# Transposes of two units in product banks, an earlier k, h blocks around the last attn x v, and new scheduler clocks, in a fused attention and MLP kernel

## The chip, the cores and the metric

The kernel runs on one core of one Trainium2 chip. The metric is the device time of one execution in microseconds (us). Each comparison runs the kernel before and the changed one in turns on the same chip.

The engines have the names of the profile: PE does the matmuls (x3600 on the page of the kernel before), ACT is the scalar engine (x373), DVE the vector engine (x515). The program gives PE's results tiles in PSUM; a "bank" here is such a tile of 2048 bytes a partition, as in `mm_tile` (512 fp32 columns).

## The reference, cut to what matters

```python
scores = q @ k.transpose(0, 1, 3, 2) / sqrt(64)        # 8 batches, 12 heads, 448 x 64
attn   = maximum(scores, 0) ** 2 / 448
x      = (attn @ v) as [3584, 768]
h      = x @ w_in                                      # 768 x 2048
out    = (maximum(h, 0) ** 2) @ w_out                  # 2048 x 768
```

## The kernel before

Work comes in units: four heads of one batch, three units per batch, 24 in all. A unit has seven score tiles of 128 x 896. PE makes scores into a "slot", which is two PSUM banks. ACT turns a slot into an `at` tile (relu, fp16), DVE squares `at`, and PE multiplies it by v. The output, xt, feeds the "h blocks": six matmuls into one product bank (`mm`). ACT or DVE copies that bank to g, and DVE squares g. The later stages use sums of weights and activations (`s`, `ws`, `x`) so as to need fewer matmuls; DVE makes these sums.

The scores need q^T and k^T. From unit 6 on a transposing DMA makes them; for units 0 to 5 PE does, with an identity matmul:

```python
def slot(dtype):                       # two slots of two banks, a third one in the first 27 us only
    ...
def pe_transpose(n):
    srcs = q16s.pop(n); ts = new_qkt(); ps = slot(FP16)
    def copy(i, eng):                  # eng 0: ACT, else DVE
        ...
    # 14 transposes of q, 14 of k, into the two banks of one slot
    ...
    if n == 3: return lambda: (copy(0, 0), copy(1, 0))
    if n > 0:  copy(0, n < 3); copy(1, n < 3)          # units 4, 5: both on ACT
```

The program for all engines is written out once, in order, by a small scheduler. It keeps two clocks: `at_pe` is its guess of how far PE is, `at_ve` the same for DVE. From these it decides where in DVE's order a square goes:

```python
def put(d):
    ready, cost, fn, _ = d.popleft()
    at_ve[0] = max(at_ve[0], at_pe[0], ready) + cost
    fn()
def fill(until):
    for d in (due, due_g):             # due: squares of at; due_g: relu and square of g
        while d and max(at_ve[0], at_pe[0], d[0][0]) + d[0][1] <= until:
            put(d)
def av_unit():                         # attn x v of a whole unit
    ...
    flush(rest=False)
    at_pe[0] += 2.65
def visit(tiles, ...):                 # scores of one or two tiles
    ...
    at_pe[0] += 0.19 + 0.38 * len(tiles)
```

Of the kernel before, what the change touches and what calls it, by code (L numbers as in the profile page):

```python
# [10 lines left out]
FP16 = mybir.dt.float16  # L11
FP32 = mybir.dt.float32
AF = mybir.ActivationFunctionType
# [4 lines left out]
def kernel(  # L18
# [9 lines left out]
    nc = tc.nc  # L28
# [13 lines left out]
    P = 128  # L42
    J = 7
# [4 lines left out]
    NF = FF // P  # L48
# [21 lines left out]
    PSUM = bass.MemoryType.PSUM  # L70
# [19 lines left out]
    def load16(n):  # L90
        tq = q16_p.tile([P, 2, J * D], FP16, name="q16", tag="q16")
        tk = q16_p.tile([P, 2, J * D], FP16, name="k16", tag="k16")
        nc.gpsimd.dma_start(out=tq, in_=heads(q, n))
        nc.gpsimd.dma_start(out=tk, in_=heads(k, n))
        q16s[n] = (tq, tk)

    def load_v(n):
        t = v_p.tile([P, 2, J * D], FP16, name="vt", tag="vt")
        nc.gpsimd.dma_start(out=t, in_=heads(v, n))
        vts[n] = t  # L100
# [56 lines left out]
    nc.vector.memset(zeros, 0.0)  # L157
    junk = const_p.tile([P, 1], FP16, name="junk", tag="junk")
    nc.scalar.activation(out=junk, in_=zeros[:, 0:1], func=AF.Relu)
    load_v(0)  # L160
    load16(1)
    load_v(1)
    load16(2)
    load_v(2)

    def sums_w1(i):
# [27 lines left out]
    def slot(dtype):  # L194
        slot_no[0] += 1
        third = not big and slot_no[0] % 3 == 2 and slot_no[0] < 29
        return (third_p if third else s_p).tile(
            [P, 2, 2048 // mybir.dt.size(dtype)], dtype, name="slot", tag="slot")
# [7 lines left out]
    def pe_transpose(n):  # L206
        srcs = q16s.pop(n)
        ts = new_qkt()
        ps = slot(FP16)

        def copy(i, eng):
            dst = ts[i].rearrange("p j c -> p (j c)")
            if eng == 0:
                nc.scalar.activation(out=dst, in_=pss[i][:, i, 0:J * P], func=AF.Copy)  # L214
            else:
                nc.vector.tensor_copy(dst, pss[i][:, i, 0:J * P])

        pss = [ps, slot(FP16) if n == 0 else ps]
        for i, src in enumerate(srcs):
            for j in range(J):  # L220
                for hh in range(2):
                    nc.tensor.transpose(  # L222
                        pss[i][64 * hh:64 * hh + 64, i, j * P:(j + 1) * P],
                        src[:, hh, j * D:(j + 1) * D], ident)
            if n == 0:
                copy(i, 1)
                warm(1)
        qkt[n] = ts
        if n == 3:
            return lambda: (copy(0, 0), copy(1, 0))  # L230
        if n > 0:
            copy(0, n < 3)
            copy(1, n < 3)
        return None


    xts: dict = {}
# [49 lines left out]
    def av_some(lag=2, most=3):  # L287
        done = 0
        while av_order and done < most:
            t = av_order[0]  # L290
            if t not in seen or seen[t] > now[0] - lag:
                break
            av_order.popleft()
            av_round(t)
            done += 1
            if t % J == J - 1:
                break
# [3 lines left out]
    def av_unit():  # L301

        n = unit[0]
        if n == NUN or seen.get(n * J + J - 1, 10 ** 6) >= now[0]:
            return
        unit[0] += 1
        flush(rest=False)
        at_pe[0] += 2.65
        b, u = divmod(n, NU)
        vt = vts[n]  # L310
        ps = slot(FP32)
        for j in range(J):
            at = ats.pop(n * J + j)
            for hp in range(2):
                r = slice(64 * hp, 64 * hp + 64)
                for hh in range(2):
                    nc.tensor.matmul(  # L317
                        ps[64 * hh:64 * hh + 64, hp, 0:S],
                        lhsT=vt[r, hh, j * D:(j + 1) * D], rhs=at[r, hh, :],
                        start=(j == 0), stop=(j == J - 1))  # L320
        if u == 0:
            xts[b] = x_p.tile([P, NM, S], FP16, name="xt", tag="xt")
        nc.scalar.activation(
            out=xts[b][:, 2 * u:2 * u + 2, :], in_=ps[:, :, 0:S],
            func=AF.Copy, scale=CX)
# [16 lines left out]
    at_pe = [0.0]  # L342
    at_ve = [0.0]
# [6 lines left out]
# [4 lines that stand above are left out]
# [6 lines left out]
    def now_ve(cost, lag=0.25):  # L360
        at_ve[0] = max(at_ve[0], at_pe[0] + lag) + cost
# [9 lines left out]
    def visit(tiles, turn=None, lag=2, most=3):  # L371
        now[0] += 1
        for t in tiles:
            if t % J == 0 and t >= NPE * J:
                prefetch(t // J + 2)
        if big:
            for t in tiles[:1]:
                score(t)
            av_unit()
            for t in tiles[1:]:  # L380
                score(t)
            at_pe[0] += 0.19 + 0.38 * len(tiles)
            for i, t in enumerate(tiles):
                square(ats[t], 0.6 + 0.85 * i)
            return
        for t in tiles:
            score(t, 2)
        later = pe_transpose(turn) if turn is not None else None
        flush()
        av_some(lag, most)  # L390
        if later:
            later()
        for t in tiles:
            square(ats[t])
        flush()
# [2 lines left out]
    gts: dict = {}  # L398
    mm_no = [0]

    def mm_tile(i=None):
        if i is None:
            mm_no[0] += 1
            i = mm_no[0] % len(big)
        return big[i].tile([P, 512], FP32, name="mm", tag="mm")

    def g_of(b):
        if b // 2 not in gts:
# [3 lines left out]
    def h_group(b, f):  # L412
        z = (b % 2) * S
        cell = [None]

        def step(m):
            def run():
                if m == 0:
                    cell[0] = mm_tile()
                nc.tensor.matmul(  # L420
                    cell[0][:, 0:S],
                    lhsT=w1[f // 4][:, m, (f % 4) * P:(f % 4 + 1) * P],
                    rhs=xts[b][:, m, :], start=(m == 0), stop=(m == NM - 1))
                if m < NM - 1:
                    return
                f0 = f - f % 2
                g = g_of(b)[:, f0:f0 + 2, z:z + S]
                if b == 0 and (f % 2 == 1 or f == 0) and f < 14:
                    nc.vector.tensor_scalar(
                        out=g[:, f % 2], in0=cell[0][:, 0:S],  # L430
                        scalar1=0.0, scalar2=None, op0=ALU.max)
                else:
                    nc.scalar.activation(
                        out=g[:, f % 2], in_=cell[0][:, 0:S], func=AF.Relu)
                flush()
                if b == 0 and f == NF - 1:
                    square(g)
                elif f % 2 == 1:
                    nc.vector.tensor_mul(g, g, g)
            return run  # L440

        return [(0.1892, step(m), m == 0) for m in range(NM)]
# [151 lines left out]
    def sums(i, rows, to):  # L594

        a1, a2 = tile_of(rows[0]), tile_of(rows[1])
        x, y = ((a2[:, LO], a2[:, HI]), (to.get(1), a1[:, LO]),
                (a1[:, LO], a2[:, LO]), (a1[:, HI], to.get(2)))[i - 1]
        to[i] = late["s"].tile([P, KH, P], FP16, name=f"s{i}", tag=f"s{i}")
        op = nc.vector.tensor_add if i == 1 else nc.vector.tensor_sub  # L600
        now_ve(0.6)
        op(to[i], x, y)  # L602

# [169 lines left out]
    NB0 = NU * J  # L773
    warm(10)
    pe_transpose(0)
    for i in range(11):
        visit([t for t in (2 * i, 2 * i + 1) if t < NB0],
              turn={1: 1, 4: 2, 10: 3}.get(i))
        if i == 0:
            load16(3)  # L780
            load_w1(0)
            load_w1(1)
            load_v(3)
        if i == 2:
            load16(4)
            load_w1(2)
            load_v(4)
        if i == 5:
            load16(5)
            load_w1(3)  # L790
            load_v(5)
    load_v(6)
    load_w2(b11, 0, 0)
    load_w2(b12, 0, 1)
# [2 lines left out]
    load_qk(6)  # L797
    load_qk(7)
    first.close()
    big.append(ctx.enter_context(tc.tile_pool(name="mma", bufs=2, space=PSUM)))  # L800


    f0 = h_group(0, 0)
    for _, fn, _ in f0[0:4]:
        fn()
    av_some(0, 9)
    rounds.close()
    big.append(ctx.enter_context(tc.tile_pool(
        name="mmb", bufs=2, space=PSUM, side="right", reuse_waits="tile")))
    visit([NB0, NB0 + 1])  # L810

    T_G = NM * 0.1892
# [31 lines left out]
    for pr in range(1, B // 2):  # L844
# [3 lines left out]
        for i in range(21):  # L848
            ts = [t0 + 2 * i, t0 + 2 * i + 1]
# [25 lines left out]
    for i in (1, 2):  # L875
        events.append((2 * T_H - (3 - i) * T_G, lambda i=i: outs[0][1](i)))

    steps = [(0.1892, None, False)] * 4 + f0[4:]
    for f in range(1, NF):
        steps += h_group(0, f)  # L880
    for f in range(NF):
        steps += h_group(1, f)
# [49 lines left out]
```

## Time and profile before

| | kernel before |
|---|---|
| median of the first three runs | 378.81 us |
| range of these | 378.57 to 378.95 us |
| span of the profiled execution | 377.6 us (its device time was 379.35 us) |
| busy: PE, DVE, ACT | 96%, 74%, 66% |

The device time is some 1.8 us more than the span (379.35 against 377.6 here). A timeline line gives the start, the duration, the engine, the source line, the operation and how many instructions were merged; the bracket gives idle time of the engine before it and what ended it. For PE the duration is modelled (the score pair of the changed kernel at 35.57 us is given 0.57 us, and the next group starts after 0.50), so the text measures from the start of one group to the start of the next. L258 is line 258 of the kernel that was profiled, so the same instruction has another line number in another kernel.

### The profile page before, as it was taken

The numbers are of one execution on the slowest core, as the hardware profiler recorded it, in microseconds if no ns is written. First come the engines' busy times: TensorE is split into PE (matmuls) and PEld (weight loads), VectorE is DVE, ScalarE is ACT, GpSimd is POOL, SyncE is SP. The second block draws the span as 40 slices with busy tenths as digits, with TensorE's granted clock in tenths as the row PEclk, the third lists the DMA queues.
The fourth block names the chain that finished last, engine by engine and source line by source line (L and its number), as shares of the span: only waits on it lengthen the run. The fifth ranks groups of instructions, "written<-read, shape, count | busy, mean of one in ns | idle before, by whom it ended". The sixth has DMA issues, their size and how long they took to land.

```text
span 377.6 us, 8806 instructions
## 1 busy us (share of the span) xinstructions
PE 363.5 (96%) x3600; PEld 231.3 (61%) x3600; DVE 278.6 (74%) x515; ACT 249.8 (66%) x373; POOL 107.1 (28%) x128
## 2 busy tenths in 40 slices
PE   7889999999999999999999999999999999999994
PEld 3544444444455678785555577877555588985663
DVE  1796567997767689897965758989956688995542
ACT  2897996686677798775566578877766785532220
POOL 8545431944440444404042243150000000000001
PEclk9999999999999999999999999999999999999998
DMA  8999999999999999789498997893132200002333
GB/s 120 197 204 205 205 203 177 124 171 134 121 139 187 134 114 139 90 95 82 96 112 134 184 178 68 83 110 63 38 97 69 76 26 2 2 0 65 94 96 84
DMA packets 121160, 42.65 MB, mean 113 GB/s; under 512 B 100832, under 2 KB 117760, under 8 KB 121120
## 3 DMA queue, kind: packets, MB, share of 16 engines
q0 software_dynamic: 82912, 23.01, 59.9%
q1 hardware_dynamic: 38048, 18.98, 26.2%
q8 instruction: 28, 0.46, 0.5%
q10 hardware_dynamic: 160, 0.10, 0.1%
q14 instruction: 12, 0.10, 0.1%
HBM read 45.61 MB, written 11.01 MB: 150 GB/s over the span
## 4 chain that ended last, share of the span: by engine, by line
PE 81%; ACT 6%; DVE 6%; issue 2%; DMA 2%; POOL 1%; POOLq 0%; ACTq 0%; DVEq 0%
PE mm L729 33%; PE mm L550 23%; PE slot L252 9%; PE mm L420 9%; PE slot L317 7%; ACT at L256 4%; DVE at L369 2%; DMA k<-in_k_dram 2%; PE slot L222 1%; DVE g L491 1%; ACT m L486 1%; DVE xt L283 1%; DVE s L602 1%; DVE g L498 0%; ACT qT L214 0%
## 5 line engine op out<-in xcount | busy, mean ns | idle before, releaser
L256 ACT ACTIVATE at<-slot 128x896 f16<-128x896 f32 x168 | 146.2, 920 | 33.0 <-PE slot L252 33.0
L369 DVE TENSOR_TENSOR at<-at 128x896 f16<-128x896 f16 x168 | 99.7, 618 | 15.7 <-ACT at L256 14.5
L108 POOL DMA_DIRECT2D qs<-in_q_dram x36 | 35.4, 984 | 121.3 <-DMA qT<-qs 113.6
L729 PEld LDWEIGHTS <-s 128*128 128x128 f16 x440 | 41.7, 98 | 32.0 <-issue 4.3
L252 PE MATMUL slot<-qT,kT 64*64 64x448 f16 x756 | 58.1, 360 | 2.6 <-ACT at L256 1.2
L550 PEld LDWEIGHTS <-w 128*128 128x128 f16 x576 | 54.4, 98 | 5.9 <-issue 5.4
L550 PE MATMUL mm<-xt,w 128*128 128x224 f16 x432 | 48.6, 259 | 0.0
L729 PEld LDWEIGHTS <-g 128*128 128x128 f16 x336 | 31.5, 98 | 24.0 <-issue 5.0
L550 PEld LDWEIGHTS <-ws 128*128 128x128 f16 x432 | 40.2, 98 | 6.7 <-issue 6.7
L729 PE MATMUL mm<-b,g 128*128 128x384 f16 x224 | 40.7, 326 | 0.0
L420 PE MATMUL mm<-xt,w 128*128 128x448 f16 x192 | 39.6, 353 | 0.3 <-ACT xt L280 0.3
L729 PE MATMUL mm<-b,s 128*128 128x384 f16 x216 | 39.6, 326 | 0.1
L729 PE MATMUL mm<-t,s 128*128 128x384 f16 x224 | 39.5, 326 | 0.0
L636 DVE SCALAR_TENSOR_TENSOR osb<-mm,u 128x384 f32<-128x384 f32 (+1 forms) x30 | 16.2, 541 | 31.2 <-ACT u L631 23.0
L252 PEld LDWEIGHTS <-kT 64*64 64x64 f16 x756 | 19.9, 104 | 31.1 <-issue 25.7
L108 POOL DMA_DIRECT2D ks<-in_k_dram x36 | 35.0, 975 | 9.9 <-DMA b<-in_moe_w_out_dram 5.8
L631 ACT ACTIVATE u<-mm 128x384 f32<-128x384 f32 x28 | 13.7, 491 | 32.6 <-PE mm L729 31.4
L571 POOL DMA_DIRECT2D out_dram<-osb x2 | 1.1, 563 | 120.5 <-DVE osb L636 120.5
L550 PE MATMUL mm<-x,ws 128*128 128x224 f16 x288 | 34.4, 259 | 0.9 <-ACT m L486 0.9
L317 PE MATMUL slot<-at,vt 64*64 64x448 f16 x588 | 32.2, 350 | 0.6 <-DVE at L369 0.5
L498 DVE TENSOR_TENSOR g<-g 128x896 f16<-128x896 f16 x48 | 29.7, 619 | 1.1 <-ACT g L501 0.2
L420 PEld LDWEIGHTS <-w 128*128 128x128 f16 x192 | 17.3, 98 | 19.1 <-issue 4.8
(66 smaller groups left out, 400.2 us busy)
## 6 DMA issues: line engine op xcount, KB each, us to landing
out_dram<-osb SPq DMA_DIRECT2D x52, 192.0 KB, 3.3
vt<-in_v_dram POOLq DMA_DIRECT2D x24, 224.0 KB, 6.6
qs<-in_q_dram POOLq DMA_DIRECT2D x36, 112.0 KB, 4.4
ks<-in_k_dram POOLq DMA_DIRECT2D x36, 112.0 KB, 5.3
w<-in_moe_w_in_dram POOLq DMA_DIRECT2D x8, 384.0 KB, 11.5
b<-in_moe_w_out_dram POOLq DMA_DIRECT2D x4, 768.0 KB, 17.1
q<-in_q_dram POOLq DMA_DIRECT2D x6, 224.0 KB, 8.3
k<-in_k_dram POOLq DMA_DIRECT2D x6, 224.0 KB, 8.6
```

What stands on the lines that cost most here:

```text
L108: nc.gpsimd.dma_start(out=t[:, :, hh, :], in_=heads(src, n)[:, hh].rearrange("p (j d) -> p j d", d=D))
L222: nc.tensor.transpose(pss[i][64 * hh:64 * hh + 64, i, j * P:(j + 1) * P], src[:, hh, j * D:(j + 1) * D], ident)
L252: nc.tensor.matmul(ps[c, hh, 0:S], lhsT=kT[r, j, c], rhs=qT[r, :, c], start=True, stop=True)
L256: nc.scalar.activation(out=at, in_=ps[:, :, 0:S], func=AF.Relu, scale=SK)
L317: nc.tensor.matmul(ps[64 * hh:64 * hh + 64, hp, 0:S], lhsT=vt[r, hh, j * D:(j + 1) * D], rhs=at[r, hh, :], start=(j == 0), stop=(j == J - 1))
L369: lambda: nc.vector.tensor_mul(at, at, at), 0))
L420: nc.tensor.matmul(cell[0][:, 0:S], lhsT=w1[f // 4][:, m, (f % 4) * P:(f % 4 + 1) * P], rhs=xts[b][:, m, :], start=(m == 0), stop=(m == NM ...
L498: due_g.append((t, 0.54, lambda: nc.vector.tensor_mul(g, g, g), b))
L550: nc.tensor.matmul(XY[s][y][:, r * Q:(r + 1) * Q], lhsT=left(k, i0 + 2 * s + r, m), rhs=right(k, m), start=(fresh and r == 0 and m == 0), ...
L631: nc.scalar.activation(out=t, in_=X[0][:, 0:HALF], func=AF.Copy, scale=CO)
L636: nc.vector.scalar_tensor_tensor(out=osb[row][:, c], in0=acc[0][:, 0:cc.stop - cc.start], scalar=CO, in1=keep[nm][:, cc], op0=ALU.mult, op ...
L729: nc.tensor.matmul(acc[0][:, 0:HALF], lhsT=left()[:, f], rhs=right[:, f], start=(fresh and f == 0), stop=(f == KH - 1), skip_group_check=n ...
```

## The change

It has three parts by intent, and a fourth that touches the scheduler's clocks. (1) q and k of unit 1 are loaded ahead of v of unit 0, so that the first transposes don't wait for k. (2) Unit 3 is transposed behind more attn x v work, and the first h blocks stand around the last attn x v, where PE waited for copies. (3) Units 4 and 5 are transposed into two product banks, so that the score slots stay free, and k^T is copied by DVE beside ACT's q^T. (4) The clocks get PE's real times, and squares that are due go ahead of the `s` sums.

```diff
+    load16(1)
     load_v(0)
-    load16(1)
+    load16(2)
     load_v(1)
-    load16(2)
     load_v(2)
 ... pe_transpose
+        if n > 3:
+            pss = [mm_tile(None, FP16).rearrange("p (i c) -> p i c", i=1) for _ in range(2)]
+        else:
+            pss = [ps, slot(FP16) if n == 0 else ps]
 ...
         if n == 3:
-            return lambda: (copy(0, 0), copy(1, 0))
+            return lambda: (copy(0, True), copy(1))
         if n > 0:
-            copy(0, n < 3)
-            copy(1, n < 3)
+            copy(0, n > 3)
+            copy(1)
 ... av_unit, visit, sums
-        at_pe[0] += 2.65
+        at_pe[0] += 1.33
-            at_pe[0] += 0.19 + 0.38 * len(tiles)
+            at_pe[0] += 0.19 + 0.19 * len(tiles)
+        while due and due[0][0] <= max(at_ve[0], at_pe[0]) + 0.3:
+            put(due)
         now_ve(0.6)
 ... main part; turn 3 goes from the last visit to behind the loop
+    later = pe_transpose(3)
 ...
-    for _, fn, _ in f0[0:4]:
-        fn()
+    av_some(1, 9)
+    some(f0[0:2])
+    later()
     av_some(0, 9)
 ...
+    some(f0[2:4])
+    some(f1[0:2])
     visit([NB0, NB0 + 1])
```

More of the change, by code (lines that the diff above doesn't have):

```diff
@@ L208, in pe_transpose, with copy @@
         ts = new_qkt()
-        ps = slot(FP16)
-        def copy(i, eng):
-            dst = ts[i].rearrange("p j c -> p (j c)")
-            if eng == 0:
-                nc.scalar.activation(out=dst, in_=pss[i][:, i, 0:J * P], func=AF.Copy)
-            else:
-                nc.vector.tensor_copy(dst, pss[i][:, i, 0:J * P])
-        pss = [ps, slot(FP16) if n == 0 else ps]
+        ps = None if n > 3 else slot(FP16)
+        def copy(i, act=False):
+            dst, ps = ts[i].rearrange("p j c -> p (j c)"), pss[i][:, i if n < 4 else 0, 0:J * P]
+            if act:
+                nc.scalar.activation(out=dst, in_=ps, func=AF.Copy)
+            else:
+                nc.vector.tensor_copy(dst, ps)
+        if n > 3:
+            pss = [mm_tile(None, FP16).rearrange("p (i c) -> p i c", i=1) for _ in range(2)]
+        else:
+            pss = [ps, slot(FP16) if n == 0 else ps]
         for i, src in enumerate(srcs):
@@ L222, in pe_transpose @@
                     nc.tensor.transpose(
-                        pss[i][64 * hh:64 * hh + 64, i, j * P:(j + 1) * P],
+                        pss[i][64 * hh:64 * hh + 64, i if n < 4 else 0, j * P:(j + 1) * P],
                         src[:, hh, j * D:(j + 1) * D], ident)
             if n == 0:
-                copy(i, 1)
+                copy(i)
                 warm(1)
@@ L229, in pe_transpose @@
         if n == 3:
-            return lambda: (copy(0, 0), copy(1, 0))
+            return lambda: (copy(0, True), copy(1))
         if n > 0:
-            copy(0, n < 3)
-            copy(1, n < 3)
-        return None
+            copy(0, n > 3)
+            copy(1)
     xts: dict = {}
@@ L387, in visit @@
             score(t, 2)
-        later = pe_transpose(turn) if turn is not None else None
+        if turn is not None:
+            pe_transpose(turn)
         flush()
         av_some(lag, most)
-        if later:
-            later()
         for t in tiles:
@@ L399, with mm_tile @@
     mm_no = [0]
-    def mm_tile(i=None):
+    def mm_tile(i=None, dtype=FP32):
         if i is None:
@@ L404, in mm_tile @@
             i = mm_no[0] % len(big)
-        return big[i].tile([P, 512], FP32, name="mm", tag="mm")
+        return big[i].tile(
+            [P, 2048 // mybir.dt.size(dtype)], dtype, name="mm", tag="mm")
     def g_of(b):
@@ L776 @@
     for i in range(11):
-        visit([t for t in (2 * i, 2 * i + 1) if t < NB0],
-              turn={1: 1, 4: 2, 10: 3}.get(i))
+        visit([t for t in (2 * i, 2 * i + 1) if t < NB0], turn={1: 1, 4: 2}.get(i))
         if i == 0:
@@ L799, with some @@
     first.close()
-    big.append(ctx.enter_context(tc.tile_pool(name="mma", bufs=2, space=PSUM)))
-    f0 = h_group(0, 0)
-    for _, fn, _ in f0[0:4]:
-        fn()
+    big.append(ctx.enter_context(tc.tile_pool(
+        name="mma", bufs=2, space=PSUM, reuse_waits="tile")))
+    f0, f1 = h_group(0, 0), h_group(0, 1)
+    def some(part):
+        for _, fn, _ in part:
+            fn()
+    av_some(1, 9)
+    some(f0[0:2])
+    later()
     av_some(0, 9)
@@ L876 @@
         events.append((2 * T_H - (3 - i) * T_G, lambda i=i: outs[0][1](i)))
-    steps = [(0.1892, None, False)] * 4 + f0[4:]
-    for f in range(1, NF):
+    steps = [(0.1892, None, False)] * 6 + f1[2:4] + f0[4:6] + f1[4:6]
+    for f in range(2, NF):
         steps += h_group(0, f)
```

## The prediction

> **What bounds the kernel now.** I read the page first: busy times, then the chain that ended last.
>
> ```profile
> PE 363.5 (96%) x3600; PEld 231.3 (61%) x3600; DVE 278.6 (74%) x515; ACT 249.8 (66%) x373; POOL 107.1 (28%) x128
> PE 81%; ACT 6%; DVE 6%; issue 2%; DMA 2%; POOL 1%; POOLq 0%; ACTq 0%; DVEq 0%
> ```
>
> PE is the bound, with 81% of the chain. The change touches about the first 60 us, so I ask for PE's busy time by stretch (columns: stretch, its length, then busy time and count per engine: PE, PEld, DVE, ACT, POOL; clock, DMA share, GB/s).
>
> ```profile
> 0.00:27.40 27.40, 22.65 (x356) 12.49 (x356) 17.16 (x32) 18.92 (x23) 16.93 (x30) 1.00 1.10 173
> 45.00:60.00 15.00, 14.54 (x140) 6.34 (x138) 10.50 (x20) 13.80 (x18) 3.87 (x4) 1.00 1.55 193
> 60.00:84.00 24.00, 23.96 (x178) 11.29 (x171) 21.65 (x32) 16.98 (x27) 13.37 (x15) 1.00 1.75 155
> ```
>
> Up to 27.4 us PE is not full: there ACT is the bound, turning 21 score tiles into `at`. From 45 to 60 us ACT is nearly as full as PE (13.80 of 15). From 60 to 84 PE is full without a gap, so time won before 60 us moves everything behind it forward. The view of who waits for whom names what the change is aimed at (us in total, times, longest):
>
> ```profile
> PE slot L222 <- ACT at L256: 1.0, 3, 0.6
> PE slot L222 <- DMA k<-in_k_dram: 0.7, 1, 0.7
> PE slot L252 <- ACT kT L214: 0.5, 2, 0.3
> PE mm L420 <- ACT xt L280: 0.3, 1, 0.3
> ```
>
> Busy time alone hides part of the loss, because matmul ends are modelled. So I work from starts in the timeline: a group's real time is the next PE group's start minus its own.
>
> [...] Seven 128-column fp16 transposes are 896 columns, 1792 bytes, so q^T fits one product bank and k^T another; before, both lie in one two-bank score slot, and there are only two such slots after the first 27 us. [...] 0.62 us on DVE, 0.92 on ACT. [...] So the place of a copy in its engine's order matters; the trace shows ACT rows in program order throughout.
>
> **The change part by part.**
>
> (1) *k of unit 1 ahead of v of unit 0.* The first loads form one stream in issue order; the landings in the trace are q0 5.12, k0 6.20, v0 7.40, q1 8.72, k1 11.45, v1 12.63 us, about 1.2 us each with one 2.7 us step at k1. What k1's lateness costs, in the timeline:
>
> ```profile
> 8.42 3.35 ACT L256 ACTIVATE at<-slot 128x896 f16<-128x896 f32 x4 [6.18 <-PE slot L252]
> 10.20 0.58 PE L222 MATMUL slot<-ident,q 128*64 128x128 f16 x14 [0.24 <-ACT at L256]
> 11.49 0.58 PE L222 MATMUL slot<-ident,k 128*64 128x128 f16 x14 [0.72 <-DMA k<-in_k_dram]
> 12.01 0.95 PE L252 MATMUL slot<-qT,kT 64*64 64x448 f16 x16
> 12.63 4.96 ACT L256 ACTIVATE at<-slot 128x896 f16<-128x896 f32 x6 [0.87 <-PE slot L252]
> ```
>
> k1 becomes the fourth load and lands at about 8.7 us (10.3 if the long step stays in that place), both before 10.78, when PE has done the q transposes. Then the k transposes start at 10.78 instead of 11.49, the scores at 11.30 instead of 12.01, and ACT's next tile at 11.92 instead of 12.63; ACT is busy to 11.77, so its gap falls from 0.87 to 0.15. Gain 0.71. ACT bounds this stage to 27.3, and its other gaps (0.34 and 0.27) come from PE waiting for ACT's slots, so they move along: the 0.71 arrives at 27.3. v0 lands at about 11.45, its first use is near 12.1, so it should not take over as a wait, with 0.6 us to spare.
>
> (2) *First h blocks around the last attn x v; q^T, k^T of unit 3 on two engines.* Before:
>
> ```profile
> 26.57 0.58 PE L222 MATMUL slot<-ident,q 128*64 128x128 f16 x14 [0.57 <-ACT at L256]
> 28.83 0.76 PE L270 MATMUL avt<-at,vt 64*64 64x448 f16 x12
> 29.42 0.55 PE L252 MATMUL slot<-qT,kT 64*64 64x448 f16 x8
> 30.22 2.81 PE L420 MATMUL mm<-xt,w 128*128 128x448 f16 x14 [0.25 <-ACT xt L280]
> ```
>
> The score group of 8 before the transposes begins at 25.27 and takes 1.30 us to the next start; undisturbed such a group takes 0.51. The group at 29.42 takes 0.80 (it ends in the wait for xt on ACT, behind both copies). With the small gaps at changes of tile form PE loses 1.67 us between 25.27 and the end of the third h block at 32.96 (7.69 us elapsed, 6.02 of work at 0.047 us per 64x64 matmul of 448, 0.189 per h matmul, 0.033 per transpose). After, 8 attn x v matmuls stand ahead of the transposes and fill 0.4 of the slot wait, and eight h matmuls stand behind the last attn x v while xt is copied, so that wait vanishes. What stays is 0.3 at the slot and some 0.65 of changes of form. Gain about 0.7.
>
> (3) *Units 4 and 5 through product banks.* Before, unit 4:
>
> ```profile
> 35.72 0.92 ACT L214 ACTIVATE qT<-slot 128x896 f16<-128x896 f16 x1 [0.49 <-PE slot L222]
> 36.53 0.91 ACT L214 ACTIVATE kT<-slot 128x896 f16<-128x896 f16 x1
> 37.50 0.38 PE L252 MATMUL slot<-qT,kT 64*64 64x448 f16 x4 [0.26 <-ACT kT L214]
> 37.81 0.87 PEld L420 LDWEIGHTS <-w 128*128 128x128 f16 x6 [0.20 <-issue]
> 39.05 0.88 PE L252 MATMUL slot<-qT,kT 64*64 64x448 f16 x8
> 39.87 0.87 PEld L420 LDWEIGHTS <-w 128*128 128x128 f16 x6 [0.20 <-issue]
> ```
>
> The first score pair behind the transposes starts at 36.85 and takes 0.96 until 37.81: its second tile belongs to unit 3 and does not need k^T, it waits for the slot that the copies still read. The next takes 0.82 (39.05 to 39.87), because ACT is late by the k^T copy. Undisturbed is 0.51, so the loss is 0.45 + 0.31 = 0.76. After, the slot is free and the first term goes. The second stays mostly: ACT must still do the g copy, then two tiles of 0.86 each, while PE reaches the second tile of the next pair 1.4 us or so after the g copy; I leave 0.2 of the 0.31. k^T on DVE stands behind two squares and a g square there, which puts its end some 2 us behind the transposes, about 1 us before the first scores of unit 4. Unit 5 (46.32 to 47.28, 48.52 to 49.34) has the same figures. Gain 2 x 0.55 = 1.1.
>
> (4) *The scheduler's clock* (1.33 and 0.19 for 2.65 and 0.38, and squares put ahead of the `s` sums). The compiled order shows PE unchanged behind 50 us; DVE only swaps neighbours: pairs of squares (1.1 us) move ahead of an `s` sum at some ten places, a few relu and square steps change places. In the trace the sums end 0.6 to 5.8 us before their products. At the tightest place (0.11 us, at 338) the order is unchanged; at the next (0.64, at 265) the sum moves forward. The remaining waits of PE behind 90 us hang on ACT copies, whose order does not change. I count 0, give or take 0.6.
>
> Sum: 0.71 + 0.7 + 1.1 = 2.5 us, 378.8 - 2.5 = 376.3 us.
>
> **The rivals.** *A: the loads take it back.* If the transfers set the pace, an earlier PE only waits. Against: k^T of unit 6, the first one made by a transposing DMA, lands at 65.91 and its first scores start at 71.05, and no later unit has less than 5 us; the last w1 part lands at 40.4 and is used near 54. If v0 landed after 12.1 it would cost part (1) up to 0.7: 377.0. *B: the copy on DVE is late*, behind two squares, and the scores of unit 4 wait for k^T instead of for the slot. For: [...] its slice from 34.8 to 37.0 is solid. Against: the 1 us worked out above. It would cost up to 1.1: 377.4. *C: DVE's new order starves something behind 84 us*, where it is 74% to 90% busy: a few waits of 0.3 to 0.6 more, 377 to 378; or fewer, 375.3. *D: the waits removed were shadows of ACT's load*, which stays nearly full from 45 to 60 us: then part (3) gives just the 0.45 twice, or less, and the total is 376.6 to 377.
>
> **Range and chances.** A 2% step is 7.6 us, three times the whole sum; all PE waits of the first 60 us together would not reach it, and no part adds work to PE. Range 375.2 to 377.6: the low end has 0.5 more from ACT's relief and 0.6 from part (4), the high end loses one whole part. Faster by 2%: 0.01; within: 0.98; slower: 0.01.
>
> **What would show each step right or wrong.** (1) No wait on k in PE's waits, ACT's gap before its fifth tile near 0.15. (2) The wait for xt on ACT gone, the third h block done near 31.5. (3) The wait for ACT kT gone, the pair behind the transposes at 0.51, the next pair near 0.7. At 62 us the same h matmul 2.5 us earlier, and the distance kept to the end. (4) is wrong if that lead grows or shrinks by over 0.6 behind 84 us. A wait on v0, on kT from DVE or on a product bank would make the prediction wrong.

The traces show:

- The changed kernel copies q^T and k^T of unit 4, 128 x 896 in fp16 (1792 bytes), each out of one product bank (`qT<-mm` at 34.05 us, `kT<-mm` at 35.68); the program gives that tile 2048 bytes.
- The figures 0.62 and 0.92 us in the prediction are copies of 896 columns out of a slot in the trace of before: its six on DVE (L216) took 0.61 to 0.63 us, its six on ACT (L214) 0.91 to 0.92.
- All 373 instructions of ACT and 515 of DVE in the trace of before, and 370 and 518 in that of the changed kernel, stand in the order of the compiled program (compared by their source lines). That is what the argument on places in an engine's order rests on.
- For the "changes of form": an h block of six between groups of another tile form takes 1.24 us (33.47 to 34.71 in the trace of before), where six times 0.189 is 1.13; 14 h matmuls in a row take 2.74 (30.22 to 32.96), where the work is 2.65. So it is some 0.1 us for a group, of six or of 14. A score pair takes 0.51 (32.96 to 33.47), where its work is 0.38.
- By the view of stretches DVE is busy 72% to 86% from 84 to 341 us in the trace of before; the 74% to 90% of rival C is a little high.

## The result, and the profile after

The changed kernel took 377.69 us (median of six, 377.66 to 378.12), the kernel before 378.69 us on the same chip (378.51 to 379.09). The ratio is 0.9975, with a 95% interval of 0.9962 to 0.9988. A ratio here is the mean time of one kernel's fast runs over that of the other's in the same rounds, so it is not quite the ratio of the medians. The change gains 1.0 us; the prediction said 2.5, with a range that ended at 377.6.

The page of the changed kernel, the lines of busy time and of the chain that ended last:

```profile
PE 363.3 (97%) x3600; PEld 231.1 (61%) x3600; DVE 280.4 (75%) x518; ACT 247.6 (66%) x370; POOL 107.2 (29%) x128
PE 80%; DVE 9%; ACT 6%; issue 2%; DMA 1%; POOLq 0%; POOL 0%; ACTq 0%; DVEq 0%
```

DVE's share of the chain has grown from 6% to 9%. Its busy time has grown by only 1.8 us, which is its three new copies of k^T (some 0.6 us each). A view by stretch shows that early on ACT has been relieved and PE is fuller (from 45 to 60 us ACT 12.83 us after 13.80 before, PE 14.69 after 14.54):

```profile
45.00:60.00 15.00, 14.69 (x144) 6.59 (x137) 9.74 (x18) 12.83 (x18) 3.87 (x4) 1.00 1.53 194
60.00:84.00 24.00, 24.00 (x175) 11.54 (x174) 23.13 (x35) 17.84 (x29) 11.17 (x12) 1.00 1.68 139
```

Part (1) in the timeline. The wait of 0.72 us before the k transposes is gone, they follow q's at once, and ACT runs from its first tile without a gap (seven tiles in one line):

```profile
8.50 5.84 ACT L258 ACTIVATE at<-slot 128x896 f16<-128x896 f32 x7 [6.26 <-PE slot L254]
10.28 0.58 PE L225 MATMUL slot<-ident,q 128*64 128x128 f16 x14 [0.24 <-ACT at L258]
10.66 0.58 PE L225 MATMUL slot<-ident,k 128*64 128x128 f16 x14
```

Part (2). The scores of unit 3 now take 0.51 us (28.80 to 29.31), since nothing waits for xt any more. The third h block ends at 31.68, so the stretch that took 7.69 us before takes 7.24 (24.44 to 31.68):

```profile
24.44 0.72 PE L254 MATMUL slot<-qT,kT 64*64 64x448 f16 x8
25.73 0.58 PE L225 MATMUL slot<-ident,q 128*64 128x128 f16 x14
28.80 0.57 PE L254 MATMUL slot<-qT,kT 64*64 64x448 f16 x8
29.31 2.44 PE L422 MATMUL mm<-xt,w 128*128 128x448 f16 x12
31.68 0.57 PE L254 MATMUL slot<-qT,kT 64*64 64x448 f16 x8
```

Part (3), unit 4. The pair of score tiles behind the transposes takes 0.50 us (35.57 to 36.07) in place of 0.96. The next pair takes 0.89 (37.31 to 38.20), not less than the 0.82 of before but more:

```profile
35.57 0.57 PE L254 MATMUL slot<-qT,kT 64*64 64x448 f16 x8
35.68 0.62 DVE L216 COPY kT<-mm 128x896 f16<-128x896 f16 x1
36.12 2.55 ACT L258 ACTIVATE at<-slot 128x896 f16<-128x896 f32 x3
37.31 0.38 PE L254 MATMUL slot<-qT,kT 64*64 64x448 f16 x4
37.89 0.38 PE L254 MATMUL slot<-qT,kT 64*64 64x448 f16 x4 [0.19 <-ACT at L258]
```

I then matched each PE group of the two traces by its place in the program and subtracted the starts. The changed kernel leads by 0.83 us at 15 us, by 1.28 at the end of the third h block, by 1.67 behind unit 4 and by 2.1 behind unit 5. This lead is constant up to 210 us, where it falls by 0.37, and near 273 us it falls by another 0.35. At the end 1.4 us are left.

Here is the first fall, in DVE's timeline. Before, an `s` sum stands ahead of two squares:

```profile
209.27 0.68 DVE L602 TENSOR_TENSOR s<-g,g 128x1024 f16<-128x1024 f16 x1
210.07 0.63 DVE L369 TENSOR_TENSOR at<-at 128x896 f16<-128x896 f16 x1
```

After, the two squares stand ahead of the sum. They are not ready (DVE idles 0.72 and 0.18 us for ACT), the sum is late, and PE's product waits for it:

```profile
207.94 0.62 DVE L371 TENSOR_TENSOR at<-at 128x896 f16<-128x896 f16 x1 [0.72 <-ACT at L258]
208.75 0.62 DVE L371 TENSOR_TENSOR at<-at 128x896 f16<-128x896 f16 x1 [0.18 <-ACT at L258]
209.29 0.68 DVE L606 TENSOR_TENSOR s<-g,g 128x1024 f16<-128x1024 f16 x1
210.03 1.47 PE L733 MATMUL mm<-b,s 128*128 128x384 f16 x8 [0.20 <-DVE s L606]
```

Near 273 us it is the other way round: PE's attn x v waits for squares that stand behind g work:

```profile
272.09 0.38 PE L319 MATMUL slot<-at,vt 64*64 64x448 f16 x4 [0.19 <-DVE at L371]
```

The waits view of the whole changed kernel shows what is new on DVE (the first of these lines was 0.5 us in two waits before, the second was not there in this form):

```profile
PE slot L319 <- DVE at L371: 0.7, 3, 0.4
PE mm L733 <- DVE s L606: 0.2, 1, 0.2
```

The gap in PE's work is larger than these figures, because the matmul before is modelled to end later than it does: from start to start, less the group's usual time, the two cost 0.37 and 0.35 us.

So three questions are left. Why do the timed runs gain 1.0 us when the traces differ by 1.4 to 1.5? Why did parts (2) and (3) bring less than predicted? And is it part (4) that takes 0.7 back?

### The profile page after: what moved, and what is told of

The parts are those of the page before. It is cut to its first block, busy times and chain, and to the rows that moved or that the text cites. A ratio compares the mean times of both kernels' runs of the same rounds, so it can differ in the third digit from the quotient of the medians.

```text
span 376.1 us, 8798 instructions
## 1 busy us (share of the span) xinstructions
PE 363.3 (97%) x3600; PEld 231.1 (61%) x3600; DVE 280.4 (75%) x518; ACT 247.6 (66%) x370; POOL 107.2 (29%) x128
## 4 chain that ended last, share of the span: by engine, by line
PE 80%; DVE 9%; ACT 6%; issue 2%; DMA 1%; POOLq 0%; POOL 0%; ACTq 0%; DVEq 0%
PE mm L733 31%; PE mm L552 22%; PE mm L422 9%; PE slot L254 9%; PE slot L319 7%; ACT at L258 5%; DVE at L371 3%; DVE g L493 1%; DVE g L500 1%; DMA q<-in_q_dram 1%; DVE s L606 1%; PE slot L225 1%; DVE osb L640 1%; DVE g L498 1%; ACT m L488 1%
## 5 line engine op out<-in xcount | busy, mean ns | idle before, releaser
L552 PEld LDWEIGHTS <-w 128*128 128x128 f16 x576 | 54.4, 98 | 5.9 <-issue 5.4
L493 DVE TENSOR_TENSOR g<-mm,m 128x448 f16<-128x448 f32 x36 | 22.0, 619 | 9.4 <-ACT m L488 4.1
```

What stands on the lines that cost most here:

```text
L493: nc.vector.tensor_add(gs(s, hi, right), acc(s, y), keep[s, nm])
L552: nc.tensor.matmul(XY[s][y][:, r * Q:(r + 1) * Q], lhsT=left(k, i0 + 2 * s + r, m), rhs=right(k, m), start=(fresh and r == 0 and m == 0), ...
```

## The experiments

### The kernel before as its own control

No edit.

> The kernel before, run again as its own control, for a second trace and the noise of a comparison. Theory 1 (the lead of 2.1 us at 60 us that the trace of the changed kernel shows is real in every run): ratio 1.000 within 0.001, and the same landings, k of unit 1 near 11.45 us, the same wait of 0.7 us. Rival (the traced run of before was a slow one, 379.35 us against a median of 378.7, so that part of the lead is only in that trace): a span 0.5 us or more below 377.6, with k of unit 1 earlier or another wait shorter, named by where the two traces of this same kernel part.

378.5 us (378.26 to 379.29) against 378.77, ratio 0.9991 (0.9974 to 1.0007), span 377.1. The rival holds. k of unit 1 landed at 11.03 us in this trace, not at 11.45, and PE lost 0.26 us there instead of 0.90. I measure that loss as the time from the start of the first q transpose to the first k transpose, less the 0.39 us that it takes undisturbed. The trace of before that the prediction rests on was a slow draw of something that varies from run to run.

### The load order alone

```diff
+    load16(1)
     load_v(0)
-    load16(1)
+    load16(2)
     load_v(1)
-    load16(2)
```

> The kernel before with the loads of q and k of unit 1 and 2 moved ahead of v of unit 0 and 1, nothing else. Theory 1: 0.7 to 0.8 us less than before (378.0), ACT's gap before its fifth tile 0.15 in place of 0.87, and the lead of 0.8 kept to the end. Rival: the late k of unit 1 is an accident of one trace; then the gain is 0.3 us or less.

378.25 us (378.13 to 378.57) against 378.77, ratio 0.9983 (0.9969 to 0.9997). The gain is 0.5 us, between the two expectations, and the runs scatter less than those of before. Five traces have the old load order (before, control and three below). In these k of unit 1 landed at 11.45, 11.03, 10.18, 10.18 and 11.80 us, and PE lost 0.90, 0.26, 0, 0 and 1.50 us: 0.53 on average, from five widely spread values. In all eight traces with the new order PE lost nothing there. The worst case is in the trace of the kernel only_blocks, told below, whose profiled run took 380.26 us:

```profile
9.96 0.58 PE L222 MATMUL slot<-ident,q 128*64 128x128 f16 x14 [0.24 <-ACT at L256]
11.85 0.71 PE L222 MATMUL slot<-ident,k 128*64 128x128 f16 x14 [1.30 <-DMA k<-in_k_dram]
```

There the loss did not end with the wait. From 12.15 to 15.57 us the granted PE clock was 0.50, where it was 1.00 in the other four traces:

```profile
12.20:15.60 3.40, 3.40 (x46) 1.68 (x44) 3.00 (x6) 1.73 (x2) 1.99 (x4) 0.51 1.26 201
```

From ACT's first score tile to its 21st this trace takes 20.63 us, 2.6 more than the 17.99 to 18.00 of the two traces that lost nothing. Counted so, the five traces lose 0.77 us on average. The length of the wait alone does not bring the slow clock: in the kernel no_sumrule, told below, it stays 1.00 behind a wait of 1.65 us. The three longest of all timed runs, 380.26 (this one), 380.27 and 381.98 us, have the lowest mean clocks (0.994, 0.995, 0.993), and all three have the old load order. That the other two lost their time in the same place is not shown, as they have no trace.

In the new order the fifth load is v of unit 0, which PE first uses at 12.05 us in the trace of only_loads and at 12.27 in that of the changed kernel. In the trace of one later kernel, split_turns, it came at 12.49 us and cost some 0.2 us of the lead; this was the first rival's wait of the prediction:

```profile
12.53 0.57 PE L288 MATMUL avt<-at,vt 64*64 64x448 f16 x8 [0.18 <-DMA vt<-in_v_dram]
```

### The scheduler's numbers and rule alone

```diff
-        at_pe[0] += 2.65
+        at_pe[0] += 1.33
-            at_pe[0] += 0.19 + 0.38 * len(tiles)
+            at_pe[0] += 0.19 + 0.19 * len(tiles)
+        while due and due[0][0] <= max(at_ve[0], at_pe[0]) + 0.3:
+            put(due)
```

> The kernel before with only the scheduler's numbers and the rule that squares go ahead of the s sums; PE and ACT orders are those of before, DVE order is that of the changed kernel apart from its three copies. Theory 1 (the lead is lost to two new waits on DVE, near 210 and 272 us, 0.36 and 0.35 us by the trace of the changed kernel): 0.7 us slower than before (379.4), and both waits in its trace. Rival (these two waits come from the earlier parts' shift, the order is harmless): same as before within 0.2 us.

379.09 us (378.8 to 381.98) against 378.77, ratio 1.0016 (0.999 to 1.0041). By time alone this is inconclusive: the sign is that of the theory, the interval includes 1, and the scatter of k of unit 1 is in both kernels. The trace is clear: the lead over the trace of before falls by 0.37 us near 210 and by 0.36 near 273 us, and nowhere else behind 20 us. So the two waits belong to part (4), without any help from the earlier parts.

### The change without the scheduler's part

The lines of the diff just shown, taken back from the changed kernel. In the compiled order DVE then differs from the kernel before by its three copies alone.

> The changed kernel with the scheduler's old numbers and without the rule for squares, so DVE's order is that of before plus three copies. Theory 1: the lead of 2.1 us at 60 us reaches the end, 376.6 us, 0.7 below the changed kernel and 2.1 below before in the trace. Rival: the waits come back elsewhere, no faster than the changed kernel (377.7).

376.97 us (376.88 to 377.23) against 378.77, ratio 0.9949 (0.9935 to 0.9963). The theory holds, though its 376.6 was 0.4 too low. The median is 0.72 us below the 377.69 of the changed kernel (timed in another comparison), and in its trace the lead stays within 0.03 us from 55 us to the end: 2.3 us, as both falls are gone. This version beats both kernels.

### The product banks alone

The edit is the diff's part on `pe_transpose` and `mm_tile`, with unit 3 as before.

> The kernel before with units 4 and 5 transposed into two product banks and copied by ACT and DVE, nothing else. Theory 1 (the slot wait behind each transposition, 0.45 us, goes; the next pair of scores loses 0.07 us more, since ACT is then the limit): 0.8 us less than before, 377.9, pairs at 0.51 and 0.89 us. Rival (the 1.1 us of the prediction were right and something else of the changed kernel took 0.3): 1.1 us less, second pair near 0.7.

378.21 us (377.38 to 379.28) against 378.69, ratio 0.9992 (0.9978 to 1.0006). The time decides nothing: it has the old load order, and its six runs scatter over 1.9 us. The trace gives the part by itself. The lead rises by 0.38 us at unit 4 and by 0.46 at unit 5, 0.84 in all (some 0.07 of the second comes at the attn x v behind it), and the pairs behind the transposes take 0.51 and 0.89 us, as in the changed kernel. So the part was worth 0.8 us, not 1.1.

### The h blocks and unit 3 alone

The edit is the main part of the diff, with k^T of unit 3 copied by DVE; units 4 and 5, the loads and the clocks as before.

> The kernel before with the first h blocks around the last attn x v and unit 3 transposed after the loop, its k^T copied by DVE; nothing else. Theory 1 (0.38 us of attn x v fill the slot wait and 0.29 us of wait for xt go, two changes of tile form cost 0.22 more): 0.45 us less than before, 378.3, and 6.0 us or less from the transposes of unit 3 to the end of the third h block against 6.4. Rival (it was worth 0.7 as predicted, and another part of the changed kernel took 0.25): 0.7 us less.

378.18 us (377.92 to 380.26) against 378.69, ratio 0.9996 (0.998 to 1.0012): inconclusive by time, for the same reason. In the trace the stretch from the last score tile before the transposes to the end of the third h block takes 7.24 us (26.76 to 34.00), exactly as in the changed kernel (24.44 to 31.68), against 7.69 before. So this part was worth 0.45 us.

### What holds the second pair of scores

To the version without the scheduler's part:

```diff
-                if b == 0 and (f % 2 == 1 or f == 0) and f < 14:
+                if b == 0 and (f % 2 == 1 or f in (0, 4, 8)) and f < 14:
```

> The changed kernel without the scheduler's numbers, and with the relu copy of the h blocks right behind the transposes of units 4 and 5 (f 4 and 8) moved from ACT to DVE. It asks what holds the second pair of scores there at 0.89 us. Theory 1 (ACT's rate: two tiles of 0.86 and some 0.43 until the first can start are 2.16 us, while PE comes back after 1.75): the pair falls only to 0.7 to 0.8, the total by 0.1 to 0.3 (376.8). Rival (the g copy in front of the two tiles holds it): the pair falls to 0.51 and the total by 0.75 (376.2).

376.92 us (376.81 to 376.99) against 378.69, ratio 0.9953 (0.994 to 0.9966). With the g copy out of ACT's way the pair takes 0.79 us in place of 0.89:

```profile
35.80 3.47 ACT L258 ACTIVATE at<-slot 128x896 f16<-128x896 f32 x4 [1.04 <-PE slot L254]
37.10 0.85 PE L254 MATMUL slot<-qT,kT 64*64 64x448 f16 x8
37.89 0.93 PE L422 MATMUL mm<-xt,w 128*128 128x448 f16 x4
```

ACT starts its first tile 0.44 us after the pair of before has started at 35.36, and two tiles last 1.73 us. So the second slot is free 2.17 us after that start, at 37.53. PE is back after 1.74 us, at 37.10, and wants that slot 0.19 later, at 37.29. That makes a wait of some 0.25 us from ACT's rate alone; the pair takes 0.28 beyond its 0.51. So the theory holds for the pair. For the total it expected 0.1 to 0.3 us less; the medians differ by 0.05 us and the traces' lead by 0.1, too little to call a gain.

### Numbers and rule apart

Two kernels complete a two by two: the changed kernel without the rule for the `s` sums, and the changed kernel with the old numbers.

> The changed kernel without the rule that puts due squares ahead of the s sums, but with the scheduler's new numbers. It tells apart which of the two makes which wait. Theory 1: the wait of PE for s near 210 us (0.36) is of the rule and goes, the wait for squares near 272 us (0.35) is of the numbers and stays; 377.3, 0.35 below the changed kernel. Rival: both waits are of one of the two, so both go (377.0) or both stay (377.7).

> The changed kernel with the scheduler's old numbers (2.65 and 0.38) but with the rule that puts due squares ahead of the s sums: the fourth of the two by two. Theory 1 (with the old numbers 376.97, with both new 377.69, with the numbers alone 378.78 and a wait of 1.81 us for squares near 273): the rule alone makes the wait for s near 210 us (0.36) and none near 273; 377.3. Rival: the rule alone does no harm, since the order near 210 also hangs on the numbers; 377.0.

| | without the rule | with the rule |
|---|---|---|
| old numbers (2.65, 0.38) | 376.97 | 377.41 |
| new numbers (1.33, 0.19) | 378.78 | 377.69 |

The four medians come from different comparisons (before was 378.77 us beside 376.97, 379.01 beside 377.41, 378.69 beside the two others). The ratios to before are 1.0003 (0.999 to 1.0016) without the rule and 0.9959 (0.9947 to 0.9972) with the old numbers. My expectation for the first failed: taking the rule away did not gain 0.35 us, it lost 1.1. Its trace shows that the wait near 210 us is gone, but the one near 273 has grown to 1.8 us. There the last square that attn x v needs stands behind two `s` sums, an output sum and g work:

```profile
271.66 0.69 DVE L604 TENSOR_TENSOR s<-s,g 128x1024 f16<-128x1024 f16 x1
272.27 1.69 DVE L371 TENSOR_TENSOR at<-at 128x896 f16<-128x896 f16 x3
272.94 0.38 PE L319 MATMUL slot<-at,vt 64*64 64x448 f16 x4 [1.65 <-DVE at L371]
```

The expectation for the second held: with the old numbers the rule alone makes the wait near 210 us (its trace loses 0.37 us against the one without the rule there, and nothing anywhere else), 377.41 us. So the new numbers spoil DVE's order near 273 us by 1.8 us. The rule was needed with them: it brings back all but 0.35 us of that, at the price of the wait near 210. With the old numbers neither is needed. Why truer times make a worse order I can only argue: with a smaller `at_pe` the scheduler takes DVE to be more behind and places squares later in the order.

### A version meant to space the score pairs

To the version without the scheduler's part:

```diff
+    # pe_half(n, i): the 14 transposes of q (i = 0) or k (i = 1), one bank, one copy
-    seq = [[2, 3], 4, [4, 5], [6, 7], [8, 9], 5, [10, 11], [12, 13], [14, 15], ...
+    seq = [[2, 3, (4, 0)], [4, 5, (4, 1)], [6, 7], [8, 9], [10], [11, (5, 0)],
+           [12, 13, (5, 1)], [14, 15], [16], [17, 18], [19], [20], []]
```

> A version meant to beat both: the changed kernel without the scheduler's numbers and rule, with the q and the k transposes of units 4 and 5 taken apart, each right behind a pair of scores, so that they space the pairs by 1.75 + 0.45 = 2.2 us against the 2.16 that ACT needs; single tiles where no transposes stand. Theory (ACT's rate behind a pair is what is left): the pairs behind them at 0.51 to 0.55 us, 0.8 to 1.0 us of waits gone, some 0.25 of new changes of form; 376.4. Rival (ACT's own sum of work up to 60 us is the limit, 13.8 busy of 15 us): the waits come back a few blocks on; 376.9 or more.

> As split_turns, with the relu copies of h blocks 4 and 8 on DVE in place of ACT. If ACT is the limit here, 0.1 to 0.3 us below split_turns; if DVE is by now as full, the same or slower.

377.31 us (377.26 to 377.59) and, with g blocks 4 and 8 on DVE, 377.40 (377.14 to 377.97), both against 379.01, ratios 0.9959 (0.9946 to 0.9971) and 0.9957 (0.9944 to 0.9971). Both beat before and miss what they were made for: by the medians they are some 0.3 to 0.4 us slower than 376.97. The lead behind 14 us ends 0.21 us lower than in the version without the scheduler's part, in both traces; split_turns lost some 0.2 us more to the late v of unit 0. The traces say where. The pair that the k transposes stand behind takes 0.50 us, as meant, but the pair after it holds a tile of unit 4, and takes 0.98 because k^T is not yet copied. One attn x v loses 0.51 us to a late square (24 of its matmuls take 1.64 us where 1.13 is usual), and each visit of a single tile makes two more changes of tile form (some 0.1 us each, an estimate from the groups timed beside the prediction). The expectation failed. The rival's time came true, but not for its reason: with two g copies taken from ACT the loss is the same 0.21 us.

## Why the prediction was wrong

The "within 2%" and the places of the first three gains were right. The size was wrong: the predicted 376.3 us missed the 377.69 by 1.4, and by its own terms this is where it went:

| step of the sum | predicted | shown | by |
|---|---|---|---|
| (1) k of unit 1 | 0.71 | 0.5 | 0.52 between medians; mean of five traces 0.53, or 0.77 with the slow clock behind one |
| (2) h blocks, unit 3 | 0.7 | 0.45 | 7.69 to 7.24 us, in two traces |
| (3) units 4 and 5 | 1.1 | 0.8 | lead in the trace of that part alone |
| (4) scheduler | 0 | -0.7 | 376.97 against 377.69; 0.37 and 0.35 in traces |
| sum | 2.5 | 1.05 | measured: 1.0 |

**Step (4) failed, and is half of the miss.** "I count 0, give or take 0.6" was wrong by 0.7. The prediction looked at the two places with the least slack (the time from the end of a sum to its product) and found those unharmed. For the others it had only the 1.1 us that a pair of squares lasts, and near 210 us the slack was 1.85. But a sum moved behind two squares doesn't lose their duration alone; it also inherits their wait for ACT, here 0.9 us (0.72 and 0.18). With PE's lead of 2.13 us counted, the sum starts 2.15 us later than before, more than the slack. The second place was missed because the prediction checked the `s` sums alone, and there the squares came late. Rival C named the kind of loss, at the size that came; it was given too little weight.

**Step (1): right mechanism, size from one draw.** The trace of before showed 0.72 us of wait, and this was taken for its constant cost. It varies, from 0 to 1.5 us in five traces, and the timed runs put the gain at 0.5. The trace of before lost 0.4 us more there than that, which accounts for the traces differing by 1.4 to 1.5 us and the timed runs by 1.0.

**Step (2): the gaps that remain were undercounted.** "What stays is 0.3 at the slot and some 0.65 of changes of form" was 0.95; it measured 1.22 (7.24 less 6.02 of work). The group of attn x v ahead of the transposes ends with 0.53 us beyond its work (24.82 to 25.73, with 0.38 of work), and splitting the h block and the attn x v adds changes between 64 x 64 and 128 x 128 tiles: two h matmuls take 0.48 us (27.14 to 27.62) where their work is 0.38, four take 0.86 (27.94 to 28.80) where it is 0.76, and the four attn x v matmuls between them 0.32 where it is 0.19.

**Step (3): right on the slot, wrong on the next pair.** The first term, 0.45 a unit, came as stated. The second, "I leave 0.2 of the 0.31", failed: the loss grew by 0.07. Taking away PE's first wait brought PE sooner to ACT, whose two tiles set the distance of pairs at some 2.17 us. This is rival D, within one pair. Rival B was ruled out: k^T was copied by 36.30, and its first use was past 37.3. Rival A happened once in eight traces, with a wait of 0.18 us.

Three things that the prediction used held in the trace of the changed kernel too: one bank took each of q^T and k^T and the slots were free (pair at 0.50 us), the copy took 0.62 us on DVE and 0.92 on ACT, and DVE's 518 instructions ran in the program's order. That order made the two new waits: at 209.29 us the sum starts behind two squares for which DVE had idled 0.72 and 0.18 us, and at 272.09 PE waits for squares that stand behind g work.

What stays open: why the fifth load is the late one (10.18 to 11.80 us in five traces with the old order; in the new one 11.43 in the changed kernel and 12.49 in split_turns), what brought the slow clock behind the worst wait, and why truer times gave the worse order. That all but 0.05 us of the sum is explained should not be read as that precision; the terms carry some 0.1 to 0.2 us each.

## What to carry to other kernels

A wait on a transfer that one trace shows may be one draw of many, so look at the scatter of the timed runs, and at a second trace of the same kernel, before pricing it. When an instruction moves behind others on an engine that runs them in order, as DVE does in both traces here (515 and 518 instructions), compare its slack with their duration plus their own waits, and do it for everything on that engine and not for one kind. A change that bundles gains with a retuned scheduler should be timed without the retuning: here the best version is the change less that part.
